# Sharing one weight load of the identity among the 16 fold matmuls of a single-token attention kernel

## The chip, the cores and the metric

The kernel runs on one core of one Trainium2 chip. The metric is device microseconds of one execution (us). "Ratio" below always means: the mean time of one kernel's fast runs over the mean time of the kernel before in the same rounds on the same chip. It is therefore not quite the ratio of the medians that are also quoted. The engines are PE (matmul), PEld (its weight loads, which overlap PE), DVE (vector), ACT (scalar) and SP (which issues the transfers).

## The reference, cut to what matters

Two independent attentions, A and B, each with one query token, 32 heads, 8192 cached keys and values per head, head size 128, all bf16:

```python
q = (x @ wq).reshape(B, Sq, H, Dh)            # one token
scores = einsum("bhqd,bhkd->bhqk", q, k_cache) * Dh ** -0.5
p = softmax(scores)
o = einsum("bhqk,bhkd->bhqd", p, v_cache)
return o.reshape(B, Sq, H * Dh) @ wo           # A and B are concatenated
```

Each k or v element is used once. So 285 MB have to come from HBM, almost all of it k_cache and v_cache.

## The kernel before

Work goes in 32 steps `j`, two heads each. k and v blocks of 4 MB land in a ring of five slots. DVE multiplies a k block in place by the broadcast query (8 instructions of 128x2048). Then the *fold* sums the 128 products of each key: PE multiplies by the identity and accumulates 16 slices of 8 columns in PSUM, and DVE reduces the 8 sums that remain. One fold is half a block, so there are 64 folds.

```python
def plan_fold(j, h):
    ...
    def op(e):
        for c in range(NF):                                   # NF = 16
            m = e.matmul(
                fold_ps[h][:, :].rearrange("p (t e) -> p t e", e=FE), ident[:],
                t[:, h * HT:(h + 1) * HT, c * FE:(c + 1) * FE],   # 512 columns
                start=(c == 0), stop=(c == NF - 1))
        m.then_inc(c_f.sem, 1)
    OP('PE', op)
    if h == 1:
        release(('k', j), (c_f, v))       # the slot is free: SP issues the next transfer

def plan_PV(j):
    ...
    for i in range(t0, t1):               # 128 matmuls, each with a v slice as weights
        m = e.matmul(ot_ps[j % 2][:, 0:2], t[:, i, :], p2[:, j % 2, i, :], ...)
# the last v block comes in four parts, and the last PV waits for each of them:
LAST_PARTS = [(0, 64), (64, 96), (96, 112), (112, 128)]
# order of transfers: wq, wq, k0, k1, v0, k2, v1, ... , k31, wo, v30, v31
# after the last k block: fold, fold, softmax, PV(30), PV(31), output product, store
```

`e.matmul` emits a weight load and a matmul each time, so the same identity is loaded 1024 times.

## Time and profile before

| | before |
|---|---|
| median of 3 runs | 684.23 us (682.97 to 684.96) |
| span of the profiled run | 680.7 us |
| PE / PEld / DVE busy | 479.8 / 264.9 / 377.8 us |
| fold matmuls, busy | 320.5 us, 484 ns each |
| fold weight loads, busy | 117.3 us, 120 ns each |
| rate of the transfers | about 430 GB/s in nearly all slices |

From the page of the kernel before, the head and two rows of the 40 slices of the span (PEclk is the granted PE clock in tenths of full speed, DMA the mean busy share of the 16 DMA engines), and the queue from which PE's instructions are fetched:

```profile
PE 479.8 (70%) x5660; PEld 264.9 (39%) x5660; DVE 377.8 (56%) x513; ACT 42.5 (6%) x169; POOL 2.4 (0%) x16
...
PEclk9998867877876867789867786967887668678885
DMA  9999999999999999999999999999999999999993
GB/s 370 431 430 431 431 433 429 429 430 430 427 435 433 428 430 432 430 426 430 431 430 429 431 430 430 428 405 432 429 432 432 428 426 430 430 430 433 422 415 131
...
q8 instruction: 44, 0.72, 0.4%
```

No engine is full, and the transfers are, from the first slice to the last but one.

From the timeline of the same run, two folds, the first at half clock and the second at full clock (start us, duration us, engine, what, count, and in brackets the idle time before it):

```profile
648.41 5.31 PE L374 MATMUL fold<-ring,ident 128*128 128x512 bf16 x16 [1.83 <-DVE ring L361]
...
649.10 0.15 PEld L374 LDWEIGHTS fold<-ring,ident 128*128 128x128 bf16 x1 [0.28 <-issue]
...
649.52 0.15 PEld L374 LDWEIGHTS fold<-ring,ident 128*128 128x128 bf16 x1 [0.27 <-issue]
...
656.47 3.13 PEld L374 LDWEIGHTS fold<-ring,ident 128*128 128x128 bf16 x16 [0.30 <-DVE ring L361]
656.47 3.63 PE L374 MATMUL fold<-ring,ident 128*128 128x512 bf16 x16 [0.22 <-DVE ring L361]
```

At half clock the load side sits idle 0.28 us between loads: it waits for the matmul, not the other way round. (The first fold ran partly at full clock.)

The end of the chain of waits of the kernel before (start us, us, what), from the last DMA piece in it to the last instruction:

```profile
605.27 38.42 DMA ring<-in_B_k_cache_dram
...
648.41 5.31 PE fold L374 x16
...
656.47 3.63 PE fold L374 x16
...
666.46 3.43 PE otps L459 x128
...
670.56 0.32 PE otps L459 x12
670.88 1.51 issue
672.39 3.25 PE otps L459 x116
```

The last k block lands at 643.7 us. From there to the end the chain names engines only: two folds, the softmax, two PVs. "issue" is time in which PE waited for nothing that the profile shows: a 1.51 us gap, 12 matmuls into the last PV.

### The profile page before, as it was taken

How to read it: one execution, taken by the hardware profiler on the slowest of the kernel's cores; microseconds unless marked ns; L12 is line 12 of the kernel's file. 1: busy time of each engine (PE TensorE's matmuls, PEld its weight loads, DVE VectorE, ACT ScalarE, POOL GpSimd, SP SyncE). 2: the span in 40 equal slices, each digit the busy share in tenths (PEclk: the TensorE clock that was granted, in tenths of full speed). 3: DMA queues.
4: the chain of work that ended last, by engine and by line, in shares of the span. 5: the costliest groups of instructions: out<-in, count | busy, mean ns of one | idle time of the engine just before them, and what ended most of it. 6: DMA issues, size and time to landing. Idle time of an engine off the chain costs nothing.

```text
span 680.7 us, 12357 instructions
## 1 busy us (share of the span) xinstructions
PE 479.8 (70%) x5660; PEld 264.9 (39%) x5660; DVE 377.8 (56%) x513; ACT 42.5 (6%) x169; POOL 2.4 (0%) x16
## 2 busy tenths in 40 slices
PE   0487877767688767856777576857768768667775
PEld 0133533434343434433433352534434234334445
DVE  4158556655555665555556526656555557463650
ACT  0110000000000000000000000000000001000000
POOL 1000000000000000000000000000000000000000
PEclk9998867877876867789867786967887668678885
DMA  9999999999999999999999999999999999999993
GB/s 370 431 430 431 431 433 429 429 430 430 427 435 433 428 430 432 430 426 430 431 430 429 431 430 430 428 405 432 429 432 432 428 426 430 430 430 433 422 415 131
DMA packets 11684, 286.01 MB, mean 420 GB/s; under 512 B 1776, under 2 KB 2288, under 8 KB 2672
## 3 DMA queue, kind: packets, MB, share of 16 engines
q1 hardware_dynamic: 11344, 285.22, 97.9%
q8 instruction: 44, 0.72, 0.4%
q14 instruction: 8, 0.07, 0.0%
q10 hardware_dynamic: 288, 0.00, 0.0%
HBM read 285.21 MB, written 0.00 MB: 419 GB/s over the span
## 4 chain that ended last, share of the span: by engine, by line
DMA 53%; PE 30%; DVE 12%; issue 3%; ACT 1%; ACTq 0%; DVEq 0%
DMA ring<-in_B_k_cache_dram 27%; DMA ring<-in_A_k_cache_dram 22%; PE fold L374 19%; DVE ring L361 11%; PE otps L459 7%; DMA xT<-in_B_x_dram 3%; PE qwps L333 2%; PE yps L537 1%; ACT qbc L340 1%; DVE m L410 1%; ACT p L429 0%; PE stps L436 0%; PE stps L405 0%; DVE wt L504 0%; PE stps L415 0%
## 5 line engine op out<-in xcount | busy, mean ns | idle before, releaser
L374 PE MATMUL fold<-ring,ident 128*128 128x512 bf16 x1024 | 320.5, 484 | 109.7 <-DVE ring L361 109.2
L361 DVE TENSOR_TENSOR ring<-ring,qbc 128x2048 bf16<-128x2048 bf16 x256 | 300.9, 1216 | 148.5 <-DMA ring<-in_A_k_cache_dram 84.9
L374 PEld LDWEIGHTS fold<-ring,ident 128*128 128x128 bf16 x1024 | 117.3, 120 | 287.8 <-issue 117.5
L459 PEld LDWEIGHTS otps<-p,ring 128*128 128x128 bf16 x4096 | 108.3, 97 | 8.7 <-issue 1.6
L459 PE MATMUL otps<-p,ring 128*128 128x2 bf16 x4096 | 108.3, 163 | 1.5 <-issue 1.5
L387 DVE TENSOR_REDUCE s_sb<-fold 128x64 f32<-128x512 f32 x64 | 43.1, 674 | 10.7 <-PE fold L374 10.3
L410 DVE TENSOR_REDUCE m<-stps 2x1 f32<-2x128 f32 x32 | 8.9, 279 | 69.8 <-PE stps L405 69.8
L436 PE MATMUL stps<-rowsum,ones_f 128*128 128x2 f32 x64 | 13.6, 282 | 41.5 <-ACT p L429 41.5
L421 ACT COPY nb<-stps 128x1 f32<-128x1 f32 x32 | 5.1, 159 | 580.3 <-PE stps L415 580.3
L333 PE MATMUL qwps<-ring,xsel 128*128 128x512 bf16 x64 | 16.7, 408 | 29.2 <-DVE xsel L226 24.3
L429 ACT ACTIVATE p<-s_sb,nb 64x128 bf16<-64x128 f32 x64 | 27.9, 436 | 2.1 <-ACT nb L421 0.3
L436 PEld LDWEIGHTS stps<-rowsum,ones_f 128*128 128x128 f32 x64 | 10.8, 211 | 44.2 <-ACT p L429 44.2
L333 PEld LDWEIGHTS qwps<-ring,xsel 128*128 128x128 bf16 x64 | 6.0, 103 | 39.4 <-issue 27.2
L415 PE MATMUL stps<-m,sel 2*128 2x1 f32 x64 | 12.3, 259 | 11.5 <-DVE m L410 11.5
L415 PEld LDWEIGHTS stps<-m,sel 2*128 2x128 f32 x64 | 9.6, 186 | 24.0 <-DVE m L410 24.0
L397 DVE TENSOR_REDUCE m<-s_sb 64x1 f32<-64x128 f32 x64 | 17.7, 277 | 1.0
L504 DVE TENSOR_TENSOR wt<-qwps,hmask 128x512 f32<-128x512 f32 (+3 forms) x5 | 2.2, 440 | 24.6 <-PE qwps L497 24.5
L429 ACT ACTIVATION_READ_ACCUMULATOR p<-s_sb,nb 64x1 f32 x64 | 11.7, 182 | 0.0
L475 DVE TENSOR_TENSOR ot<-otps,rinv 128x2 bf16<-128x2 f32 x32 | 4.9, 154 | 11.8 <-PE otps L459 11.8
L537 PE MATMUL yps<-w_bf,ring 128*128 128x1 bf16 x240 | 8.7, 172 | 1.9 <-issue 1.9
L537 PEld LDWEIGHTS yps<-w_bf,ring 128*128 128x128 bf16 x240 | 8.6, 118 | 1.9 <-issue 1.9
L405 PE MATMUL stps<-ident_f,m 128*2 128x128 f32 x32 | 8.8, 275 | 0.0
(30 smaller groups left out, 34.4 us busy)
## 6 DMA issues: line engine op xcount, KB each, us to landing
ring<-in_A_k_cache_dram SPq DMA_DIRECT2D x16, 4096.0 KB, 37.1
ring<-in_A_v_cache_dram SPq DMA_DIRECT2D x16, 4096.0 KB, 31.0
ring<-in_B_k_cache_dram SPq DMA_DIRECT2D x16, 4096.0 KB, 37.8
ring<-in_B_v_cache_dram SPq DMA_DIRECT2D x15, 4096.0 KB, 31.9
ring<-in_A_wq_dram SPq DMA_DIRECT2D x1, 4096.0 KB, 12.5
ring<-in_B_wq_dram SPq DMA_DIRECT2D x1, 4096.0 KB, 21.9
ring<-in_A_wo_dram SPq DMA_DIRECT2D x1, 4096.0 KB, 36.5
ring<-in_B_wo_dram SPq DMA_DIRECT2D x1, 2048.0 KB, 20.2
```

Source lines behind the costliest of these rows:

```text
L333: m = e.matmul(qw_ps[:, :].rearrange("p (j d) -> p j d", d=Dh), xsel[:, a, c, par, :], wq[:, c, 4 * g:4 * g + 4, par, :], start=(i == 0), ...
L361: m_val[(j, i)] = INC('DVE', c_m, lambda e: e.tensor_tensor(t, t, qbc[:, a, jj:jj + 1, :].broadcast_to([P, CH, Dh]), ALU.mult))
L374: m = e.matmul(fold_ps[h][:, :].rearrange("p (t e) -> p t e", e=FE), ident[:], t[:, h * HT:(h + 1) * HT, c * FE:(c + 1) * FE], start=(c == ...
L387: r_val[(j, h)] = INC('DVE', c_r, lambda e: e.tensor_reduce(s_sb[:, j % 2, h * HT:(h + 1) * HT], fold_ps[h][:, :].rearrange("p (t e) -> p ...
L397: m1_val[j] = INC('DVE', c_m1, lambda e, h=h, q0=q0, q1=q1: e.tensor_reduce(m1[q0:q1, j % 2, h:h + 1], s_sb[q0:q1, j % 2, :], AX.X, ALU.max))
L405: tr_val[j] = INC('PE', c_tr, lambda e: e.transpose(st_ps[j % 2][0:2, 0:P], m1[:, j % 2, :], ident_f[:]))
L410: m2_val[j] = INC('DVE', c_m2, lambda e: e.tensor_reduce(m2[0:2, j % 2:j % 2 + 1], st_ps[j % 2][0:2, 0:P], AX.X, ALU.max))
L415: bc_val[j] = INC('PE', c_bc, lambda e: e.matmul(st_ps[j % 2][:, P:P + 1], sel2[:], m2[0:2, j % 2:j % 2 + 1], start=True, stop=True))
L429: e_val[j] = INC('ACT', c_e, lambda e, h=h, q0=q0, q1=q1: e.activation(p2[q0:q1, j % 2, :, h], s_sb[q0:q1, j % 2, :], AF.Exp, bias=nb[q0:q ...
L436: s_val[j] = INC('PE', c_s, lambda e: e.matmul(st_ps[j % 2][:, P + 2:P + 4], ones_f[:], rowsum[:, j % 2, :], start=True, stop=True))
L459: m = e.matmul(ot_ps[j % 2][:, 0:2], t[:, i, :], p2[:, j % 2, i, :], start=(i == 0), stop=(i == TP - 1))
L537: m = e.matmul(y_ps[:, b:b + 1], wo[:, h0 + i, :, b], src[:, a, h0 + i:h0 + i + 1], start=(first and i == 0 and b == 0), stop=(lastblk and ...
```

## The change

The 16 matmuls of a fold have the same stationary operand. The change emits the load with the first one only; the other 15 are matmul instructions with the load left out.

```diff
+        def held_matmul(e, out, lhsT, rhs, start, stop):
+            return e.add_instruction(mybir.InstMatmult(
+                name=nc.get_next_instruction_name(), engine=e.engine,
+                ins=[e.lower_ap(rhs), e.lower_ap(lhsT)], outs=[e.lower_ap(out)],
+                start_tensor_calc=start, stop_tensor_calc=stop,
+                tile_size=(P, P), tile_position=(0, 0), ldweights=False))
 ...
                 for c in range(NF):
-                    m = e.matmul(
+                    m = (e.matmul if c == 0 else held_matmul)(
+                        *((e,) if c else ()),
                         fold_ps[h][:, :].rearrange("p (t e) -> p t e", e=FE), ident[:],
```

The intent: 960 of 5660 weight loads fewer.

## The prediction

> **What bounds the kernel now.** The transfers. The slices show DMA at 9 in 39 of 40 slices and about 430 GB/s in nearly all; part 3 shows 285.2 MB. 285.2 MB at 430 GB/s is an estimate of 663 us of the 680.7 us span. The chain of waits agrees: between each pair of folds and the next lies a piece "DMA ring<-k_cache" of 35 to 40 us, 53% of the chain in all.
>
> The chain also lists "PE fold 19%", but those folds only release a ring slot, and the transfer put into it has a long queue before it: a 4 MB k transfer takes 37 us from issue to landing (part 6), while 4.19 MB at 430 GB/s is 9.8 us. So about 27 us of transfers are already queued when a fold frees its slot.
>
> **What the change removes.** 960 of 5660 weight loads (15 of 16 in each of 64 folds); 117.3 us x 15/16 = about 110 us of weight-load busy, so the load row should fall from 265 to about 155 us. It adds and moves nothing.
>
> **What that is worth on PE.** Almost nothing. In the timeline a fold at full clock is 16 matmuls in 3.63 us; with 0.379 us for the last one, a pitch of 217 ns, and the loads (95 ns) lie inside it. At half clock the loads start every 425 to 427 ns, last 152 ns and then the load side idles 0.28 us: again the matmul sets the pitch. The Trainium skill, "TensorE: Matmul & The Clock Gate", Back-to-back issue gap, gives N/2.4 + 2.5 ns = 216 ns and N/1.2 = 427 ns for 512 columns, with no term for the load; the trace agrees with both. So the loads are already hidden behind the preceding matmul and fold time should stay near 320 us, 484 ns each, apart from how the clock happens to fall (granted mean 0.79).
>
> **Instruction fetch.** The instruction queue moved 0.72 MB; 960 fewer instructions at 64 B (16 KiB per 256 instructions, "Runtime: NRT & Kernel Launch", Instruction fetch mechanics; the trace's 44 packets for 11,320 PE instructions agree) is 61 KB, about 4 packets of some 1.07 us on one of 16 engines: 0.2 us; expect 40 packets.
>
> **On the critical path.** Only the tail after the last v part is exposed: PV, the output product, the store, 10 us in all, with no fold in it. A 1.5 us "issue" gap stands in the last PV, 12 matmuls in, not at a boundary of the v parts; I take it for a fetch of instructions. With 960 fewer instructions before it the block boundary falls elsewhere, so the tail may move by up to about 1 us either way. The last v part lands around 674 us, which limits the gain.
>
> **Prediction.** 684.0 us, range 681.3 to 686.5. Same 0.97, faster 0.015, slower 0.015. Result correct.
>
> **What would show each step.** Right: still 430 GB/s; load row about 155 us, fold loads 64; fold burst at full clock still 3.6 us, at half clock still 427 ns pitch; k transfers still about 37 us to landing. Wrong: full-clock fold bursts clearly under 3.5 us (loads were not hidden); a lower granted clock and longer folds (loads counted as activity); fewer GB/s.
>
> **What would make it wrong.** The held matmuls running slower than paired ones, enough (over 25 us late) to empty the queue; weight-load reading of on-chip memory having slowed the DMA writes, so that 430 GB/s rises; or a chip with another DMA rate.

## The result, and the profile after

The first comparison gave 681.55 us (680.75 to 682.13, 4 runs) against 684.6 us (682.97 to 685.27, 4 runs, the three above among them): ratio 0.9958, interval 0.9936 to 0.998. By the 2% rule this is "same"; the result is correct, and 681.55 us lies inside the predicted range of 681.3 to 686.5, though only 0.25 us from its edge.

From the page of the kernel after, the same rows:

```profile
PE 466.9 (69%) x5660; PEld 152.8 (22%) x4700; DVE 377.4 (55%) x513; ACT 42.5 (6%) x169; POOL 2.4 (0%) x16
...
PEclk9998868767888768778987676867887877778875
DMA  9999999999999999999999999999999999999993
GB/s 370 432 432 431 431 429 431 431 431 430 434 429 432 429 431 430 431 431 431 429 431 430 430 432 431 431 402 432 432 432 430 428 429 431 431 431 431 421 415 135
...
q8 instruction: 41, 0.67, 0.4%
```

The load row fell by 112 us, as costed. The transfer rows did not move.

From the timeline of the kernel after, a fold at full clock (the first matmul has its load, the 15 that follow are held):

```profile
640.64 0.10 PEld L382 LDWEIGHTS fold<-ring,ident 128*128 128x128 bf16 x1 [0.30 <-DVE ring L369]
640.64 0.39 PE L382 MATMUL fold<-ring,ident 128*128 128x512 bf16 x1 [0.22 <-DVE ring L369]
640.87 3.40 PE L167 MATMUL fold<-ring,ident 128*128 128x512 bf16 x15
```

From 640.64 to 644.27 is 3.63 us, to the hundredth what it was. I also took the distances between the starts of consecutive fold matmuls out of both traces: the median is 216 ns at full clock and 427 ns at half clock, before and after alike. The loads had been hidden completely.

The end of the chain of waits of the kernel after:

```profile
606.97 37.08 DMA ring<-in_B_k_cache_dram
...
649.14 4.92 PE fold L167 x15
...
657.43 4.47 PE fold L167 x15
...
667.99 3.43 PE otps L468 x128
...
672.09 3.43 PE otps L468 x128
```

The last k block lands at 644.05 us, no earlier than before. The second fold happened to run mostly at half clock (5.1 us with its first matmul, against 3.63 us), and the gap in the last PV is gone. In these two profiled runs the one cancelled the other: the spans are 680.7 and 680.4 us.

So three things were to be settled. Is the 0.4% real? Does the gap matter? And were the loads hidden, or only off the critical path?

### The profile page after: what moved, and what is told of

The parts are those of the page before. It is cut to its first block, busy times and chain, and to the rows that moved or that the text cites. A ratio compares the mean times of both kernels' runs of the same rounds, so it can differ in the third digit from the quotient of the medians.

```text
span 680.4 us, 11397 instructions
## 1 busy us (share of the span) xinstructions
PE 466.9 (69%) x5660; PEld 152.8 (22%) x4700; DVE 377.4 (55%) x513; ACT 42.5 (6%) x169; POOL 2.4 (0%) x16
## 4 chain that ended last, share of the span: by engine, by line
DMA 54%; PE 30%; DVE 12%; issue 2%; ACT 1%; ACTq 0%; DVEq 0%
DMA ring<-in_B_k_cache_dram 28%; DMA ring<-in_A_k_cache_dram 22%; PE fold L167 17%; DVE ring L369 11%; PE otps L468 7%; DMA xT<-in_B_x_dram 3%; PE qwps L341 2%; PE fold L382 2%; PE yps L546 1%; ACT qbc L348 1%; DVE m L419 1%; PE stps L414 0%; DVE wt L513 0%; ACT p L438 0%; DVE xsel L234 0%
## 5 line engine op out<-in xcount | busy, mean ns | idle before, releaser
L414 PEld LDWEIGHTS stps<-ident_f,m 128*2 128x2 f32 x32 | 2.7, 84 | 157.2 <-issue 157.2
L382 PEld LDWEIGHTS fold<-ring,ident 128*128 128x128 bf16 x64 | 6.4, 101 | 136.2 <-DVE ring L369 132.6
```

Of the source, the lines that this page charges most:

```text
L382: m = (e.matmul if c == 0 else held_matmul)(*((e,) if c else ()), fold_ps[h][:, :].rearrange("p (t e) -> p t e", e=FE), ident[:], t[:, h * ...
```

## The experiments

Twelve kernels ran, in three groups; the kernels of a group shared one chip and the runs of the kernel before.

### Group 1: is there a gain, and is it the gap in the last PV?

The theories: **A**, the gain sits in the tail, where a boundary of instruction fetch moved out of the last PV; **B**, fewer loads let transfers or folds run faster; **C**, scatter between runs. The kernel before had a median of 682.84 us here (11 runs, 681.76 to 685.33).

**before_copy**: the kernel before, no edit.

> Null test: the kernel before, unchanged. Every theory: ratio 1.000, interval within 0.998 to 1.002. If the ratio itself lies 0.3% off, the 0.4% gain of the change is not to be told from the scatter between rounds.

Measured: 683.64 us, ratio 1.0002, interval 0.9981 to 1.0024. The method shows no bias, but six runs do not resolve much below 0.2%.

**after_copy**: the changed kernel, no edit.

> The changed kernel once more. Theory A (the gain is real and sits in the tail after the last transfers: no fetch gap in the last PV any more): ratio 0.996 to 0.999, and no gap over 1 us inside the last PV. Theory B (fewer weight loads let the transfers or the folds run faster all along): the same ratio, but the last k block lands over 1 us earlier than at 643.7 us. Theory C (scatter): ratio 0.999 to 1.001.

Measured: 682.45 us, ratio 0.9991, interval 0.9972 to 1.0009. So most of the 0.4% of the first comparison did not come back, which points to scatter; the two intervals overlap. The last k block again landed at 644.0 us, and the last PV had no gap.

**before_pad64**: the paired loads stay, and 32 tiny matmuls (64 PE instructions) run while PE is idle at the start, so that PE's instructions stand to the 256-instruction blocks in the tail as in the changed kernel.

```diff
+        W('PE', c_init, n_pad)
+        def pad_op(e):
+            for _ in range(32):
+                e.matmul(qw_ps[:, 0:1], ones_b[:], ones_b[:, 0:1], start=True, stop=True)
+        OP('PE', pad_op)
         for a in range(NA):
             for g in range(GQ):
                 plan_q(a, g)
```

> The kernel before with 32 tiny matmuls (64 PE instructions with their loads) at the start, while PE is idle anyway; all 1024 fold loads stay. It gives the tail the same position against blocks of 256 instructions as the changed kernel has. Theory A: the gap after 12 matmuls of the last PV is gone, about 1.5 us less, ratio 0.996 to 0.999, like the changed kernel. Theory B and C: ratio 1.000, since no load was removed.

**after_pad192**: the changed kernel with 96 such matmuls (192 instructions), which puts the boundary back to where it was.

```diff
+            for _ in range(96):
+                e.matmul(qw_ps[:, 0:1], ones_b[:], ones_b[:, 0:1], start=True, stop=True)
```

> The changed kernel with 96 tiny matmuls (192 PE instructions) at the start; the tail has the position of the kernel before. Theory A: the gap of about 1.5 us comes back about 12 matmuls into the last PV, ratio about 1.000. Theory B: still 0.996, since the loads are still gone. Theory C: 1.000, with or without the gap.

The last two PVs in the chains of waits, first of before_pad64:

```profile
668.56 3.43 PE otps L459 x128
...
672.65 3.43 PE otps L459 x128
```

then of after_pad192:

```profile
665.03 3.43 PE otps L468 x128
...
669.13 0.32 PE otps L468 x12
669.44 1.40 issue
670.84 3.25 PE otps L468 x116
```

The place of the gap follows the count of instructions. Sixty-four instructions that do nothing took it away from the kernel that keeps all its loads, and 192 brought it back, exactly 12 matmuls in, to the kernel that has dropped them. The output product in the middle of the run confirms the count without any padding: its gap stands after 33 matmuls before and after 62 matmuls after. By then 38 folds have run, 38 x 15 = 570 loads are missing, and 570 modulo 256 is 58 instructions, or 29 pairs. This agrees with the Trainium skill, "Runtime: NRT & Kernel Launch", section Instruction fetch mechanics, which has the fetch go in blocks of 256 instructions.

The records of queue q8 confirm that the gap is a fetch. In the kernel before a packet runs from 669.89 to 670.91 us, the gap begins at 670.88, and PE goes on at 672.39 us; in the output product the packet runs from 404.40 to 405.50 us and PE goes on at 406.73 us. Not every fetch stops PE: in the kernel after one runs from 672.37 to 673.33 us, in the last PV, which has no gap.

The times did not follow, though. before_pad64: 683.41 us, ratio 1.0002 (0.9984 to 1.0021), where theory A wanted up to 0.996 to 0.999. after_pad192: 682.62 us, ratio 0.9988 (0.9967 to 1.0009), where theory A wanted 1.000. So theory A is right about what makes the gap, and these runs do not bear it out on the time: no difference that goes with the gap shows. All that group 1 shows of the total is this: the 12 runs with held loads have a mean of 682.5 us, the 23 runs with paired loads (11 of the kernel before, 6 and 6 of the two variants) 683.4 us, with standard deviations of 0.9 and 1.0 us. The difference is 0.9 us with a standard error of 0.34 us (0.91 squared over 12 plus 1.02 squared over 23, then the root). I grouped the runs after having seen them, so this is a hint of 0.1%, not a proof.

### Group 2: hidden, or only off the critical path?

Here every k and v block after the first five transfers only a quarter of itself, so that engines and not transfers are the limit (the pages show a mean of 170 to 178 GB/s in place of 420).

```diff
+                elif n >= NS:
+                    land_of[(kind, idx)] = dma(ring[:, s, 0:SLOT // 4], src[:, 0:SLOT // 4], s_slot[s])
                 else:
                     land_of[(kind, idx)] = dma(ring[:, s, :], src, s_slot[s])
```

**before_quarter**

> Wrong result on purpose: every k and v block after the first five transfers only its first quarter, the rest of the slot is old data. All the instructions of the engines stay, so the engines are the limit, no longer the transfers. Estimate from the profile: DVE busy 378 us plus exposed parts of the chain of one block pair, 400 to 500 us in all. This is the base for the next run.

**after_quarter**

> The same with held loads. Theory H (the loads were already hidden behind the matmuls, so there was no gain to lose): within 1% of the run with paired loads, a fold at full clock still 3.6 us. Theory O (the loads cost PE time, but off the critical path under the transfers): clearly faster, up to 64 folds times 15 loads of 95 ns, an estimate of 90 us at most, and fold spans shorter.

**before_quarter_5loads**

```diff
                 for c in range(NF):
+                    for _ in range(4):
+                        e.ldweights(ident[:])
                     m = e.matmul(
```

> The paired kernel with a quarter of the transfers and four more loads of the identity ahead of each fold matmul (five in all). Theory H with a load costing about the 25 ns at which a PV pair follows another: five take 125 ns[...], so nothing changes. If a load occupied its side for the 95 ns of its record, five would take 475 ns and each full-clock fold about 7.6 us in place of 3.6 us, some hundred us or more in all.

Measured: 562.52 us (558.99 to 566.37) with one load, 572.55 us (562.62 to 580.93) with held loads, 552.46 us (550.75 to 554.09) with **five** loads for each fold matmul. More loads made the kernel faster, which neither theory had. The base itself was missed: before_quarter was expected at 400 to 500 us. So was the time that theory H expected of held loads, within 1% of one load: the medians are 1.8% apart, with three of the four held runs slow; the one fast run had 562.62 us. The granted clock goes with these times. The clock row and the fold group of before_quarter:

```profile
PEclk9999898969697878889796785989898889696785
...
L376 PE MATMUL fold<-ring,ident 128*128 128x512 bf16 x1024 | 286.9, 444 | 30.0 <-DVE ring L363 29.9
```

and of before_quarter_5loads, with the group of the four extra loads:

```profile
PEclk9999899699969997899789686899789989967995
...
L378 PE MATMUL fold<-ring,ident 128*128 128x512 bf16 x1024 | 269.6, 424 | 36.5 <-DVE ring L363 36.2
...
L377 PEld LDWEIGHTS <-ident 128*128 128x128 bf16 x4096 | 232.4, 100 | 49.2 <-DVE ring L363 33.3
```

The fold matmuls start 216 ns apart at full clock and 427 ns at half clock in all three traces, five loads included; only the number of them at each clock differs. So theory H holds in what it says of the loads, though not in its time: they were hidden, and five fit under a matmul too. "Off the critical path" (theory O, up to 90 us) falls.

**after_tail**: the changed kernel with work moved out of the stretch after the last k block.

```diff
             if c:
                 plan_ri(j - 1)
+            if j == NPR - 1:
+                ys = list(perm_l)
+                for _ in range(2):
+                    plan_y(LA, *ys.pop(0))      # 96 matmuls of the output product
             plan_fold(j, 1)
 ...
         plan_exp(j)
+        plan_PV(j - 1)                          # under the softmax, was after it
         plan_sum(j)
```

> The changed kernel with PE work moved out of the stretch after the last k block has landed: 96 of the output-product matmuls go between the last two folds, and the PV before the last goes under the softmax of the last pair. If that stretch is bound by the chain of engines: the last PV starts 2 to 3 us earlier and the time falls by 1 to 2 us until the last v part (about 674 us) limits it, ratio 0.997 to 0.999. If it is bound by the last v part: no change, ratio as the changed kernel.

Measured: 683.89 us, ratio 1.0003 (0.9985 to 1.002): a miss. From its timeline, where the 96 matmuls and the second fold stand, and the last PV:

```profile
656.45 3.33 PE L546 MATMUL yps<-w_bf,ring 128*128 128x1 bf16 x96
...
660.02 4.83 PE L167 MATMUL fold<-ring,ident 128*128 128x512 bf16 x15
...
672.86 0.53 PE L546 MATMUL yps<-w_bf,ring 128*128 128x1 bf16 x12 [1.52 <-issue]
...
673.52 3.74 PE L468 MATMUL otps<-p,ring 128*128 128x2 bf16 x128
```

I had put the 96 matmuls behind the softmax of the step before, which PE waits for in order; they filled no idle time but pushed the second fold from 656.8 to 659.6 us. The moved PV won some of it back, and a gap of 1.52 us appeared in a new place. The last PV began 1.6 us later than in the kernel after (671.95 us), not 2 to 3 us earlier. The run says nothing about a tail that really is shorter.

### Group 3: do loads raise the clock, and what do many loads cost under full transfers?

The theories: **P**, loads count as activity for the throttle of the PE clock; **N**, the clock wanders by itself. The kernel before had 684.32 us here (11 runs, 681.61 to 685.24).

**before_quarter_again** and **after_quarter_again** repeat the pair of group 2 with more rounds.

> The kernel before with a quarter of the transfers once more (wrong result on purpose), to repeat the first comparison with more rounds. Base of the next two runs: about 562 us, granted clock about 0.853. Theory P (weight loads count as activity for the throttle, so fewer loads mean a lower granted clock) and theory N (the clock wanders by itself) expect the same here.

> The held loads with a quarter of the transfers once more. Theory P: clock about 0.835 to 0.845 and 568 to 575 us, slower than the run before it in the mean. Theory N: the mean of all rounds within 1% of the run before it, clock the same within 0.005. Both: a fold at full clock stays at 3.6 us.

**before_quarter_2loads**: as with five, but one extra load (`range(1)`).

> Two loads ahead of each fold matmul in place of one, a quarter of the transfers, wrong result on purpose. Theory P: clock between those of one load (0.853) and five (0.892), time between 552 and 562 us. Theory N: about 562 us, clock 0.853, and the 0.892 of five loads was something else than the number of loads.

**before_5loads**: five loads, all transfers, correct result.

> The kernel before with all transfers, correct, and four more loads of the identity ahead of each fold matmul: 4096 loads more where the change took 960 away. If transfers bound the kernel and loads are hidden, ratio 0.998 to 1.002 although the load busy rises by over 100 us; theory P: granted clock above 0.81 (0.79 before). If loads in number slow the transfers, fewer GB/s than 430 and a ratio above 1.01.

Measured, with both groups put together (clock is the mean over the runs):

| quarter transfers | runs | median us | range us | clock |
|---|---|---|---|---|
| held, group 2 / 3 | 4 / 6 | 572.55 / 566.89 | 551.93 to 580.98 | 0.837 / 0.846 |
| one load, group 2 / 3 | 4 / 6 | 562.52 / 562.62 | 558.99 to 567.20 | 0.853 / 0.851 |
| two loads, group 3 | 5 | 549.94 | 548.61 to 552.24 | 0.878 |
| five loads, group 2 | 4 | 552.46 | 550.75 to 554.09 | 0.893 |

Two loads against one in the same rounds: ratios to the kernel before of 0.804 (0.802 to 0.806) and 0.8241 (0.8209 to 0.8272). Intervals far apart, and the fold pitch the same 216 and 427 ns; in the profiled runs 201 of the distances between fold matmuls within a fold were over 350 ns, that is at or near half clock, with two loads, 244 with one (before_quarter_again). The clock row and the fold group of before_quarter_again:

```profile
PEclk9999899898969697878879586787887969896895
...
L376 PE MATMUL fold<-ring,ident 128*128 128x512 bf16 x1024 | 282.8, 439 | 30.0 <-DVE ring L363 30.0
```

and of before_quarter_2loads:

```profile
PEclk9999899969899797898988686989789869997995
...
L378 PE MATMUL fold<-ring,ident 128*128 128x512 bf16 x1024 | 274.3, 429 | 30.8 <-DVE ring L363 30.5
```

So theory P is borne out for *more* loads: extra loads bring more full-clock time, and the edit adds nothing but loads. The time, 549.94 us, lay even below the 552 to 562 us that it forecast. By what path a load raises the clock is not shown. For *fewer* loads it is not settled. All but two of the ten held runs are marked slow by the rule of 1.5% above the fastest run of the same kernel, and what they show is mainly a wide spread (551.93 us at a clock of 0.867 to 580.98 us at 0.826). Theory P has the direction of the medians, but after_quarter_again (566.89 us, clock 0.846) lies just outside what P expected (568 to 575 us, 0.835 to 0.845) and within what N allowed (1%, 0.005); the two fast held runs, 551.93 and 562.62 us, are no slower than those with one load. Five loads had a higher clock than two and no better time; why is open.

before_5loads: 687.01 us (685.55 to 688.38), ratio 1.0042 (1.0022 to 1.0062), clear of one, where I had expected 0.998 to 1.002 or over 1.01. Under full transfers, extra loads *cost* 0.4%, at a clock of 0.802 (0.797 in before_copy), so not much warmer; theory P had expected over 0.81. The end of its chain of waits says where:

```profile
652.02 26.03 DMA ring<-in_B_v_cache_dram
678.05 0.05 issue
678.10 0.60 PE otps L461 x16
```

Here the last part of the last v block, landing at 678.05 us, ends the chain. Now to why it landed so late. Each transfer raises its semaphore in 16 steps. The Trainium skill, "DMA: Bandwidth & Descriptors", section Why a DMA increments its semaphore by 16 and not by 1, gives the reason: up to 16 engines finish independently, and each posts one step when its share has landed. The traces record the time of each step, and I took them out for the last part of the last v block:

| kernel | PE instruction packets | first step us | mean us | last step us |
|---|---|---|---|---|
| before | 44 | 664.7 | 669.6 | 674.9 |
| before_copy | 44 | 664.9 | 669.7 | 674.6 |
| before_pad64 | 45 | 664.5 | 669.4 | 675.0 |
| after | 41 | 664.8 | 669.4 | 673.7 |
| after_copy | 41 | 664.9 | 669.4 | 673.6 |
| after_pad192 | 41 | 664.0 | 668.6 | 672.6 |
| after_tail | 40 | 664.7 | 669.2 | 673.2 |
| before_5loads | 60 | 665.1 | 671.4 | 678.0 |

Six or seven steps come by 666 us in every run, whatever the number of loads. The last step moves with the number of packets that fetch instructions: 672.6 to 673.7 us with 40 or 41, 674.6 to 675.0 us with 44 or 45, 678.0 us with 60. Only the large step is safe, though: for the last k block the last step comes 8.6 to 9.0 us after the first where 36 or 37 packets had run by then, 8.4 to 9.1 us with 40, and 11.6 us with 55. The distance between first and last step is not made at the end: in the kernel before it is 0.8 us for the first transfer, 3.7 us at 256 us, and 8.7 us at 548 us; with five loads 0.3, 5.3 and 10.0 us at the same places. Some of the 16 steps fall behind bit by bit, and they do so where packets are fetched. With five loads PE's first fetch packet starts at 50.3 us. Between the transfers whose first steps come at 41.9 and 51.7 us, the last of the 16 steps moves from 0.55 to 1.79 us behind the first, and the other 15 stay below 0.55 us. In the kernel after the first packet starts at 64.8 us, and the same jump (0.66 to 1.86 us) comes between the transfers at 61.3 and 71.0 us. From the transfer at 32 us to the one at 635 us the lags of the 16 steps together grow by 69.3 us in the kernel before, over 45 instruction packets (40 of PE and 5 of 8 KB in queue 14), and by 91.0 us with five loads, over 60. That is 1.5 us for each packet in both, more than the 1.06 us that one of PE's packets itself takes, and it accounts for nearly all of the lag. The ends agree too: relative to the first step, the 16 steps of before_5loads are together 23 us later than those of before (16 x (671.44 - 665.07) against 16 x (669.64 - 664.73)), and its fetch packets took 17.2 us more. The trace does not record which engine a packet ran on, so that the step which jumps is that of the engine which carried the fetch is inferred from these times, not shown.

## Why the prediction was right or wrong

**Right: the transfers bound the kernel**, and the time stayed within 0.5%. The slices are 9 and about 430 GB/s before and after.

**Right: the loads were hidden.** 112 us of load busy went away; the pitch stayed 216 and 427 ns, a full-clock fold 3.63 us, and the fold matmuls together 320.5 us before and 320.9 us after. The Trainium skill, "TensorE: Matmul & The Clock Gate", section Back-to-back issue gap, gives N/2.4 + 2.5 ns and N/1.2 for the isolated case, 216 and 427 ns for 512 columns, and the traces agree. Group 2 shows that this was no gift of the transfers: with engines as the limit, paired and held loads have the same pitch.

**Right, with a wrong weight: the gap is an instruction fetch.** Padding took it away and brought it back on call, and a fetch packet stands at it. But "the tail may move by up to about 1 us either way" is not what set the time: moving the gap alone changed nothing that six runs resolve.

**Wrong: "Only the tail after the last v part is exposed ... with no fold in it."** The chain of the kernel before says otherwise. Its last DMA piece is the last *k* block, at 643.7 us; after it come two folds, the softmax and two PVs, 33 us of engine time, while the remaining transfers (wo, v30, v31) need until 674.9 us. In the profiles of the first comparison and of group 1 the last PV ends 0.8 to 3.2 us after the last landing, and in none of them does the chain wait for a v block, so the last two folds do count: each took 3.6 us at full clock and up to 6.3 us in the profiled runs, as the clock fell. after_pad192 had the gap *and* the shortest span of group 1 (679.3 us), because its last fold ran at full clock and its last k block landed at 642.9 us. This luck is larger than the effect of the change.

**Mis-sized: "0.2 us" for the fetch of instructions.** I divided the packets' time by 16 engines. A landing counts when the *slowest* engine is done. A packet held one landing step back by about 1.5 us, not by a sixteenth of its length. The last v part landed 1.0 to 1.2 us earlier in the profiled runs with 41 packets than in those with 44 (673.7 against 674.9, 673.6 against 674.6 us), though the last k block did not, and 3.2 us later with 60. It ends the chain of waits in the profile of before_5loads alone. It is not shown to have saved any for the change: in the profile after, the last PV ends 1.8 us after that landing, so the engine chain, not the landing, ended that run, and so it was in the other profiles under full transfers with one load or held loads. The 0.9 us of group 1 has no cause shown.

**Luck in the number.** The first comparison, 2.45 us under the forecast of 684.0, fell inside the range by only 0.25 us, and the later runs repeat little of its gain. The mechanism was confirmed by the transfers and the pitch, not by how near the number came.

What stays open: whether the true gain is 0.1% or nothing (the three ratios of the held kernels are 0.9958, 0.9991 and 0.9988, two of the three intervals include one, and after_tail, held too but with its other edit, had 1.0003), and which engines lag. No version was clearly faster than both kernels.

## What to carry to other kernels

Weight loads that start inside the matmul before them cost no PE time in this kernel, though their row showed 117 us; read the distance between matmul starts, not the busy sums. When transfers are the limit, look for what makes the *last landing* later, and count instructions among it: here each packet of them went with a lag of 1.5 us in the steps of the landings. And before explaining a difference of a few tenths of a per cent, run the unchanged kernel under another name.

## What the Trainium skill lacked or had wrong

- "TensorE: Matmul & The Clock Gate", Part 1, says that the clock follows how busy PE has been, but not whether weight loads count. Here one extra load per matmul raised the granted clock from 0.851 to 0.878 and cut the engine-bound time by 2.4% (0.804 over 0.8241).
- The same page, Back-to-back issue gap, gives about 131 ns per 512-column matmul as the sustained figure in streams of load and matmul, and calls the 216 ns formula isolated. The pitch was 216 ns, with no load, one, two or five loads for each matmul.
- The same page, LDWEIGHTS, gives columns over 1.2, 107 ns for 128 columns. The records here are of that order (95 to 152 ns), but as a cost it misleads, even halved for the fast weight load that the page describes further down: five loads fit into one 216 ns pitch.
- "Runtime: NRT & Kernel Launch", Instruction fetch mechanics, calls the cost of crossing a block "mostly hidden". With the DMA engines full, streams of short PE instructions stood still for 0.7 to 3.2 us at some of these boundaries (0.72 us in before_5loads at 509 us, 3.23 us in before_copy at 403 us).
- No page read says that instruction fetch makes some DMA engines lag behind the others: first and last step of one transfer were 0.8 us apart at the start, 10.2 us at the end, and 13.0 us with 4096 more PE instructions; the lags of the 16 steps together grew by 1.5 us for each fetch packet.
